# A fifth expert in the early stage, and GpSimd's work in the written order of a spectral layer with a mixture of experts

## The chip, the core and the metric

The kernel runs on one core of one Trainium2 chip. The metric is the device time of one execution in microseconds (us), the median of several runs. TensorE (PE) does the matrix products, VectorE (DVE) and ScalarE (ACT) the elementwise work, GpSimd (POOL) issues the indirect transfers (gather and scatter of rows), and SyncE (SP) issues nearly all other transfers.

## What is computed

The reference, cut to what matters. The input x has 8 sequences of 1856 rows of 256 values; there are 4 groups of 4 experts.

```python
X = np.fft.rfft(x, axis=1); Xr, Xi = X.real, X.imag
Yr = Xr @ w_r - Xi @ w_i + b_r
Yi = Xr @ w_i + Xi @ w_r + b_i
Yr, Yi = soft_threshold(Yr, 0.01), soft_threshold(Yi, 0.01)
y = np.fft.irfft(Yr + 1j * Yi, n=1856, axis=1).reshape(14848, 256)
g = argmax(y @ w_group); e = argmax(y @ w_expert[g])        # one expert of 16 for each row
out[row] = softmax_g[g] * softmax_e[e] * (relu(y[row] @ w1[g, e]) @ w2[g, e])
```

## The kernel before

Everything is done in 32-bit values. Most products are split: a value is cut into a high part (ScalarE, a cast) and a low part (VectorE, value minus high part), and three products are added up.

**First stage: four pairs of sequences.** For each pair the transforms are done as products with small tables. One letter of the string `ORDER` stands for one step of one generator, and the steps are issued in the order of the letters. `c` and `d`: first matmuls and their transposes (the first pair's eight are issued ahead of `ORDER`, by `lead_mm` and `turn_a`). `e` (`f_mm`): eight groups of matmuls with the table `T`, then `f` and `h`, the copies of the high and the low part. `j`, `k` (`m_mm`, 12 matmuls of 512 columns with the split weights `wh` and `wl`), `m`, `n`, `o`: the bias, the products and the soft threshold, fifteen of each for a pair. `r` and `s`, `v`, `w` and `x`: the inverse transform (`b_mm`, `b_turn`, `p_mm`, `p_out`, `p_turn`), which stores rows to the DRAM tensor `ys_d`. `G`, `H`, `R`: the logits and the routing, done on VectorE, twice for a pair. `S`: one scatter by GpSimd of 128 list entries to the DRAM tensor `lst`, which has a list of rows for each expert; a routing call releases 16 of them, 128 in all. From the 65th on a scatter waits for the landing of the one five before it.

**Early jobs, in the same string.** While the last pairs are still worked on, some experts take their first rows from lists that are already long enough. `l` loads raw weights (and x of the later pairs), `W` and `V` split them. `I` and `Z` load and convert the lists, `F` gathers 256 rows into a tile `xg` (two indirect transfers on GpSimd), `T` transposes them on TensorE, `X` and `Y` copy high and low part into `xth` and `xtl` of the pool `mp`. `U`, `A`, `B` are quarters of the up product and its two copies, `D`, `E`, `J` halves of the down product of 128 rows and its two copies out of PSUM, and `K` stores 128 rows to the output by an indirect transfer. `L` loads the last lists, once all scatters have landed, and `M` gathers the 384 rows of the first late job. Before, the early jobs are 8: two of 256 rows for each of the experts 0 to 3.

**The queues.** The order of TensorE, ScalarE, VectorE and SP is that of the steps (a manual schedule). GpSimd is left to the framework's scheduler. The tiles that `F` and `X` fill (`xp2`, `mp`) are allocated once the forward pools, `T` among them, are closed, which is behind the last `o`.

**Late stage.** A list of jobs is worked on one after the other: `("e", q)` is 512 rows of expert q, `("l", q)` the 384 rows behind them, `("f", i)` a flexible job of 128 rows and `("h", i)` a half job of twice 64 rows for whatever is left in the lists. Weights lie in the ring `big` (three buffers): those of the last three early experts are kept from the early stage, all others are loaded (two loads of 1 MB) and split by eight pieces on ScalarE and VectorE (`split_w`), one or two jobs ahead, as `split_at` says. In a job of kind e or l one piece follows each of eight up groups. In a half job the code is

```python
drain(half_mm(x2, wt, hts)); next(rest, None)
half_tr(hts[0], 0, hs);      next(rest, None)
half_tr(hts[1], 1, hs)
...
emit(todo, len(todo))        # all pieces of a split that falls into this job
...
x2 = half_prep(nxt) if jobs[i + 1][0] == "h" else prep(xq, nxt, jids[i + 1].n * 128)
```

where `prep` transposes the next job's rows and copies them to `xth` and `xtl`. The first thing that the next job does on TensorE is the down product of the job before.

Of the kernel before, what the change touches and what calls it, by code (L numbers as in the profile page):

```python
# [37 lines left out]
jejleffhlhekefnhmkojkfnhmojcfnhkmddjocfnhkmddjocfnhcmdkdjddokfnhmjocnmcdjcddcddeddedfohekkfnhmojkfnhmjokfnhmjokfmhnojkfn  # L38
hmjoenmefojheekkfnhmjokfnhmjokfnhmjokfnhmjorfmhnksjsorfnhmkjssormnjokssrnmojesscffdcdlhvhxcwxwkddddcnmcdljcddvlddvwxkdwo
wxxxwcmvndvdjowcxxwldGwdvxxwxvwHwRvxwxexwxeRffhwhwkxRRRRRRRGRfhnmRRjoRRRRkRHRRRRRRRkfnhmjoRRmkRnRjRoRRenRmSRRojefRfehSRh  # L40
RRkRRSRRRRRSRkRfRRmhnRRSojRkfRRnRhSmRRjkofSnhmojSRrmnojSRkssSRrmRRSnRRjesSseffRhSRkohSrfmShnksjSsorSfnhmeSsjscSovddkwSxx
# [1157 lines left out]
```

## Time and profile before

| | us |
|---|---|
| median of 3 runs | 1142.23 |
| lowest and highest | 1140.64, 1142.94 |
| the profiled execution | 1140.41 |
| its span, first to last instruction | 1138.6 |
| TensorE busy | 1102.5 |
| VectorE, ScalarE, GpSimd busy | 663.6, 547.2, 403.3 |

The time of an execution is the span and some 1.8 us around it. Busy times are those of the profiled execution. An engine's idle time counts only where another engine, and in the end the last instruction, waits for it.

### The profile page before, as it was taken

Reading aid. Unit: us, or ns where it says so; the run is one execution under the profiler, and the core shown is the slowest. Engines: PE = TensorE matmul, PEld = TensorE weight load, DVE = VectorE, ACT = ScalarE, POOL = GpSimd, SP = SyncE. Lnnn points to the kernel's source line nnn. Section 1 sums busy time; section 2 is a strip of 40 time slices with the busy share of each in tenths; the row PEclk is TensorE's granted clock in tenths of the full one; section 3 lists DMA queues with packets and bytes.
Section 4 is the critical chain, followed back from the end, with each engine's and each line's share of the span. In section 5 each row is a group of like instructions: output and inputs, shape, how many; then the busy total and the mean of one; then the engine's idle time right before and its main releaser. Section 6 shows DMA issues by size and latency. Waiting matters only on the chain. (4 is left out here: it accounts for less than half of the span.)

```text
span 1138.6 us, 19713 instructions
## 1 busy us (share of the span) xinstructions
PE 1102.5 (97%) x7282; PEld 897.1 (79%) x7282; DVE 663.6 (58%) x1453; ACT 547.2 (48%) x1234; POOL 403.3 (35%) x462
## 2 busy tenths in 40 slices
PE   8999999999997999799999999999999999999996
PEld 5686586676684789689898898888979888798785
DVE  4635777786876795265747464464554645454452
ACT  3556455545753444134636453463544645444352
POOL 3000014414447377634242333333334333343321
PEclk9999999999999999889999999999999999999999
DMA  9500610450601840413333254335425355245300
GB/s 383 173 1 1 232 65 2 141 157 2 197 28 20 230 143 24 125 47 130 129 101 123 106 190 186 122 118 204 171 75 167 121 178 183 79 170 190 117 25 24
DMA packets 42500, 138.88 MB, mean 122 GB/s; under 512 B 17462, under 2 KB 19772, under 8 KB 32034
## 3 DMA queue, kind: packets, MB, share of 16 engines
q1 hardware_dynamic: 21602, 89.22, 22.6%
q0 software_dynamic: 15904, 31.48, 8.9%
q10 hardware_dynamic: 4896, 16.91, 4.4%
q8 instruction: 58, 0.95, 0.4%
q14 instruction: 40, 0.33, 0.1%
HBM read 103.49 MB, written 35.00 MB: 122 GB/s over the span
## 5 line engine op out<-in xcount | busy, mean ns | idle before, releaser
L526 PE MATMUL py<-big,hh 128*128 128x512 f32 x824 | 298.7, 403 | 0.0
L465 PE MATMUL ph<-xth,big 128*128 128x384 f32 (+1 forms) x896 | 257.1, 363 | 5.6 <-ACT xth L452 5.6
L527 PE MATMUL py<-big,hl 128*128 128x256 f32 x824 | 232.0, 282 | 0.0
L240 POOL DMA_INDIRECT lst<-ent,sloti x128 | 129.2, 1009 | 254.0 <-DVE mx_g L156 140.8
L471 DVE SCALAR_TENSOR_TENSOR hl<-ph,hh 128x256 fp32r<-128x256 f32 x448 | 151.3, 379 | 66.1 <-ACT hh L469 64.7
L465 PEld LDWEIGHTS ph<-xth,big 128*128 128x128 f32 x896 | 166.9, 190 | 23.8 <-ACT xth L452 6.0
L526 PEld LDWEIGHTS py<-big,hh 128*128 128x128 f32 x824 | 155.3, 189 | 37.8 <-issue 3.2
L469 ACT ACTIVATE hh<-ph 128x256 fp32r<-128x256 f32 x448 | 133.9, 351 | 71.4 <-PE ph L465 70.4
L465 PE MATMUL ph<-xtl,big 128*128 128x384 f32 (+1 forms) x448 | 162.9, 364 | 0.1
L512 POOL DMA_INDIRECT out_dram<-yo,si_f x93 | 95.0, 1022 | 178.5 <-DVE yo L534 160.3
L432 POOL DMA_INDIRECT xg<-ys_d,gi_f x93 | 90.5, 973 | 186.3 <-PE pg L448 163.5
L527 PEld LDWEIGHTS py<-big,hl 128*128 128x128 f32 x824 | 155.1, 188 | 0.1
L534 DVE SCALAR_TENSOR_TENSOR yo<-py,ent_f,yo 128x256 f32<-128x256 f32 x93 | 45.0, 484 | 168.0 <-ACT yo L533 168.0
L533 ACT ACTIVATE yo<-py,ent_f 128x256 f32<-128x256 f32 x93 | 44.1, 474 | 194.1 <-PE py L527 194.1
L415 DVE TENSOR_TENSOR big<-xt,big 128x512 fp32r<-128x512 f32 x160 | 108.8, 680 | 0.0
L414 ACT CAST big<-xt 128x512 fp32r<-128x512 f32 x160 | 99.5, 622 | 0.0
L625 PE MATMUL pw<-wh,xh 128*128 128x512 f32 x240 | 98.6, 411 | 0.0
L625 PE MATMUL pw<-wl,xh 128*128 128x512 f32 x240 | 95.0, 396 | 0.0
L465 PEld LDWEIGHTS ph<-xtl,big 128*128 128x128 f32 x448 | 85.2, 190 | 8.0 <-DVE xtl L453 0.5
L609 DVE TENSOR_TENSOR xl<-bank,xh 128x512 fp32r<-128x512 f32 x60 | 40.9, 693 | 44.5 <-PE pw L625 25.0
L597 PEld LDWEIGHTS bank<-T,big 128*128 128x128 f32 x480 | 58.5, 197 | 9.4 <-issue 3.2
L625 PE MATMUL pw<-wh,xl 128*128 128x512 f32 x240 | 65.8, 396 | 0.0
(197 smaller groups left out, 1609.1 us busy)
## 6 DMA issues: line engine op xcount, KB each, us to landing
xt<-in_w_dram SPq DMA_DIRECT2D x48, 1024.0 KB, 5.0
ys_d<-ysb ACTq DMA_DIRECT2D x32, 512.0 KB, 5.1
big<-in_w_dram SPq DMA_DIRECT2D x16, 1024.0 KB, 8.3
big<-in_x_dram SPq DMA_DIRECT2D x8, 1024.0 KB, 9.4
xt<-in_x_dram SPq DMA_DIRECT2D x8, 1024.0 KB, 6.5
lst<-ent,sloti POOLq DMA_INDIRECT x128, 3.3
lst<-zero SPq DMA_DIRECT2D x1, 1920.0 KB
xg<-ys_d,gi_f POOLq DMA_INDIRECT x93, 2.8
```

Source lines behind the costliest of these rows:

```text
L240: ins = nc.gpsimd.indirect_dma_start(out=lst, out_offset=bass.IndirectOffsetOnAxis(ap=sl_, axis=0), in_=en_, in_offset=None, bounds_check= ...
L414: nc.scalar.copy(out=wt[:, 2 * i, cs], in_=raws[i][:, cs])
L415: nc.vector.tensor_tensor(out=wt[:, 2 * i + 1, cs], in0=raws[i][:, cs], in1=wt[:, 2 * i, cs].bitcast(F32), op=ALU.subtract)
L432: ins = nc.gpsimd.indirect_dma_start(out=xg[:, c, :], out_offset=None, in_=ys_d[0:rows, :], in_offset=bass.IndirectOffsetOnAxis(ap=ids.gi[ ...
L465: nc.tensor.matmul(o[:, :n], lhsT=a_[:, ch, fs], rhs=b_[:, ch, 0:n], start=k == 0, stop=k == 5)
L469: nc.scalar.activation(out=hh[:, f, :m], in_=ov, func=AF.Relu)
L471: nc.vector.scalar_tensor_tensor(out=hl[:, f, :m], in0=ov, scalar=0.0, in1=hh[:, f, :m].bitcast(F32), op0=ALU.max, op1=ALU.subtract)
L512: ins = nc.gpsimd.indirect_dma_start(out=out, out_offset=bass.IndirectOffsetOnAxis(ap=ids.si[:, t:t + 1], axis=0), in_=ysb, in_offset=None ...
L526: nc.tensor.matmul(o, lhsT=hh[:, f, ts], rhs=w2b[:, :, f, :], start=f == 0, stop=f == 7, skip_group_check=True)
L527: nc.tensor.matmul(o[:, 0:D], lhsT=hl[:, f, ts], rhs=w2h[:, f, :], start=False, stop=f == 7, skip_group_check=True)
L597: nc.tensor.matmul(o.rearrange("p (j c) -> p j c", j=4)[:, :, m * 32:m * 32 + 32], lhsT=zys[pr][:, k, bt, :, kp], rhs=T[:, 2 * k + kp, :], ...
L625: ins = nc.tensor.matmul(y, lhsT=a_[:, c * 128:c * 128 + 128], rhs=w_[:, c // 2, c % 2].rearrange("p j e -> p (j e)"), start=False, stop=a ...
```

## The change

Expert 4 becomes the fifth early expert: two more early jobs of 256 rows (`NE2`), with its weights and lists. In the late stage its 512-row job goes, the kept weights are those of experts 2, 3 and 4, so that the late jobs of experts 0 and 1 load theirs again, and the flexible and half jobs are laid between the others by a written table (`fill`). GpSimd joins the manual schedule while `ORDER` is worked through, so its instructions too come in the order of the letters. `ORDER` itself is new. The table `T` gets a pool of its own that is closed behind the last `e`, and `xp2` and `mp` are allocated there, on the other side of the memory. At the start x of the first pair is loaded in halves, all loads are issued by SP with the constants `K` last, the table is loaded and copied in other slices, part of the weights' copies moves from ScalarE to VectorE and GpSimd, and the very first `m_mm` uses `wl` last.

```diff
@@ -35,18 +35,19 @@
 ORDER = """
...
-xRRvRSmRRnRvxwokjSxwxwRwxSRRGmRnRojRRIRRReRRHRReRfRRfhhZkRRRfkRmhnRojRkRfRmhnRSRojRkmRSRnRRSRjRRRoSemRnRSRReofRfShjhkSRR
-RRRSRRRRkRSfmhnSojRSkmnSoSRmRnSRoRSrRRFRRssrSSsSTsXSYrSUsSsrASBSUsWWSsWUASWVvABSWBUWxSwVWDxASVWBwvSVDxlwSxwVvESVvxwSxwDx
-FwVwDxVJGlEKJKITHvXRRYRvwxUxwRZRwxUAxwBFURARBRDRAFRBURRRRRvFARRBvwxxDwxwRDwxRWRRDWRRRWWTGWVFXVWYWVWVEVlEJRRJUKRRKRUARBTR
-AUBFRRUHARBDSARVRXBSTRRDYSRRRURERSRDRASVRRRURSRRRDRRAFRRRTEWBWSBUWVWJSlUJAVSBDAVXBSYDVSVDESJWDWVSWVUWVSEVJUSABRRSAURBKUR
-ARKRRDXBKAYTBUKRRSDABSDEJSUSUABSDASBUESJTXDSAYBUSUSABSDABSUEJSUABSDAXBSDYSUEJKDAKBDKUKLEJUAKBDABUMDABDEJDKDEJKDEJK
...
+xRRvRmRSRnRvRxwkwoxSwxjxwRSRGmRnRRRojRRRRIReHRRReRfRRfRhZRhkRRRRRefRmShnRRkSRRojRRSRRRRSRkfRmhSnRRojSRkfRRmShnRRRSjRokRf
+RSmhnRRSjkomSnSojRSRmeRnSRfohFRkRRRRSmSnoSTrXSYSUsSsrABSUsSsrSABSUsSsrASBSUsWWSsWDASWBvWVWSVvwxWDSxWxwVSvwVwxFlDwxExwvVV
+DwxxwVGEVIJlJKKTHvXRRZYRvwxUxwFRRwxUAxwBFURARBRDRARFBURRRRvRARRBvwxxDwxwRDwxRWRRDWRRRWWTGWVFXVWYWVWVEVlEJRRJUKRRKRUARBTR
+AUBFRRUHARBDSARVRXBSTRRDYFRRRURERRDRASVRRRURSRRRDRRASRRRTSWWBEFBUWVWJlUJAVSBDAVXBSYDVSVDElSJWUWVSWVUAVSWBDVSAlBUSEWJWVSU
+AVWBSRRADRXKWBRDRWKRWRDWKRRWYUVSEVJSUVAVSBDAVBSUEVJSUABSTATXDSBYFUDABSUEJSUABSDASBUSTADSXBYSDSUSDAKBUKUAKBDAKLEBUJEKJDAK
+XBDYEJKUMUABDABUEJUKABTADXBYDUEJKUABDABUUABDABDEJKDDEJKDDEJKDEJK
 """
@@ -265,7 +266,7 @@
-    NF = 3
+    NF, NE2 = 3, 5
...
@@ -286,10 +287,10 @@
     cA = cf.tile([128, 64], F32, name="cA")
-    nc.scalar.dma_start(out=cA, in_=cst[:, _OFF["A"][0]:_OFF["A"][0] + 64])
-    nc.scalar.dma_start(out=K, in_=cst[:, CK0:CK1])
-    nc.vector.tensor_copy(out=base, in_=kc("EB"))
-    T = cf.tile([128, K1, 128], F32, name="T")
+    nc.sync.dma_start(out=cA, in_=cst[:, _OFF["A"][0]:_OFF["A"][0] + 64])
+    table_t = ExitStack()
+    ct = table_t.enter_context(tc.tile_pool(name="ct", bufs=1, side="right"))
+    T = ct.tile([128, K1, 128], F32, name="T")
     nc.gpsimd.memset(T, 0.0)
...
@@ -302,7 +303,8 @@
         for dc in range(4):
-            ins = nc.sync.dma_start(out=t[:, dc], in_=x_v[pr, dc])
+            for rs in ((slice(0, 16), slice(16, 32)) if pr == 0 else (slice(0, 32),)):
+                ins = nc.sync.dma_start(out=t[:, dc, rs], in_=x_v[pr, dc, :, rs])
         xbig[pr] = t
...
@@ -347,19 +349,20 @@
     traw = xp.tile([128, K1, 64], F32, name="xt")
-    nc.sync.dma_start(out=traw.rearrange("p k c -> p (k c)"), in_=cst[:, 0:CF1])
+    nc.sync.dma_start(out=traw[:, 0:12].rearrange("p k c -> p (k c)"), in_=cst[:, 0:12 * 64])
     def t_blocks(k):
...
-    t_blocks(slice(0, 6))
-    craw = wf.tile([128, 2 * D], F32, name="rn", bufs=1)[:, 0:128]
-    nc.sync.dma_start(out=craw, in_=cst[:, CF1:CI0])
-
+    t_blocks(slice(0, 12))
     wraw = xp.tile([128, 2, 2, D], F32, name="xt")
...
     nc.sync.dma_start(out=bias, in_=bri)
+    nc.sync.dma_start(out=traw[:, 12:].rearrange("p k c -> p (k c)"), in_=cst[:, 12 * 64:CF1])
+    craw = wf.tile([128, 2 * D], F32, name="rn", bufs=1)[:, 0:128]
+    nc.sync.dma_start(out=craw, in_=cst[:, CF1:CI0])
+    nc.sync.dma_start(out=K, in_=cst[:, CK0:CK1])
     x1 = load_x(1)
...
@@ -367,12 +370,19 @@
                             op=ALU.subtract)
-    for w_ in (wh, wl):
-        nc.scalar.activation(out=w_[:, 1, :, 0], in_=w_[:, 0, :, 1].bitcast(F32), func=AF.Copy, scale=-1.0)
-        nc.scalar.copy(out=w_[:, 1, :, 1], in_=w_[:, 0, :, 0].bitcast(F32))
-    t_blocks(slice(6, 18))
-    t_blocks(slice(18, 30))
-    nc.scalar.copy(out=sl, in_=craw)
+    with tc.issue_after(a_last.ins):
+        nc.vector.tensor_scalar_mul(out=wh[:, 1, :, 0], in0=wh[:, 0, :, 1].bitcast(F32), scalar1=-1.0)
+        nc.vector.tensor_copy(out=wh[:, 1, :, 1], in_=wh[:, 0, :, 0].bitcast(F32))
+    nc.gpsimd.tensor_scalar_mul(out=wl[:, 1, :, 0], in0=wl[:, 0, :, 1].bitcast(F32), scalar1=-1.0)
+    w_last = nc.gpsimd.tensor_copy(out=wl[:, 1, :, 1], in_=wl[:, 0, :, 0].bitcast(F32))
+    behind_w = ExitStack()
+    behind_w.enter_context(tc.issue_after(w_last.ins))
+    sl_in = nc.gpsimd.tensor_copy(out=sl, in_=craw)
+    behind_w.enter_context(tc.issue_after(sl_in.ins))
+    t_blocks(slice(12, 21))
+    t_blocks(slice(21, 30))
+    nc.gpsimd.tensor_copy(out=base, in_=kc("EB"))
+    behind_w.close()
     nlam = cf.tile([128, 1], F32, name="nlam")
...
@@ -540,7 +550,7 @@
     yp, early = [], {}
-    jobs = [(0, 0), (0, 1), (1, 0), (1, 1), (0, 2), (1, 2), (2, NF), (3, NF)]
+    jobs = [(0, 0), (0, 1), (1, 0), (1, 1), (0, 2), (1, 2)] + [(j, e) for e in range(NF, NE2) for j in (2, 3)]
     rows = [(NP - 2) * PAIR + 1] + [(NP - 1) * PAIR + 1] * 3
...
@@ -570,7 +580,7 @@
                 yield
-        for e in range(NF + 1):
+        for e in range(NE2):
             for i, src in enumerate((w1, w2)):
...
@@ -619,11 +629,11 @@
         y = psum["m", pr, k]
-        for a_, ws in ((xh, (wh, wl)), (xl, (wh,))):
+        for a_, ws in ((xh, (wh, wl)), (xl, (wh,))) if pr + k else ((xh, (wh,)), (xl, (wh,)), (xh, (wl,))):
             for c in range(4):
...
                     ins = nc.tensor.matmul(y, lhsT=a_[:, c * 128:c * 128 + 128], rhs=w_[:, c // 2, c % 2].rearrange("p j e -> p (j e)"),
-                                           start=False, stop=a_ is xl and c == 3, skip_group_check=True)
+                                           start=False, stop=a_ is (xl if pr + k else xh) and c == 3, skip_group_check=True)
         pace[:] = pace[-1:] + [ins.ins.name]
...
@@ -729,14 +739,14 @@
-    @steps_of(range(NF + 1), range(2), range(4))
+    @steps_of(range(NE2), range(2), range(4))
     def w_high(e, i, c):
...
-    @steps_of(range(NF + 1), range(2), range(4))
+    @steps_of(range(NE2), range(2), range(4))
     def w_low(e, i, c):
...
@@ -747,11 +757,12 @@
     def list_load(j):
-        lists[j] = t = list_tiles("ab"[j], 6 + 4 * j)
+        lists[j] = t = list_tiles("ab"[j], 6 + 8 * j)
         nc.sync.dma_start(out=t.ent[:, 0:6].rearrange("p (e c) k -> p e c k", e=NF), in_=list_rows(0, NF, j * LEV, LEV))
...
             for h in range(2):
-                nc.sync.dma_start(out=t.ent[:, 6 + 2 * h:8 + 2 * h].unsqueeze(1), in_=list_rows(NF, 1, h * LEV, LEV))
+                nc.sync.dma_start(out=t.ent[:, 6 + 4 * h:10 + 4 * h].rearrange("p (e c) k -> p e c k", e=2),
+                                  in_=list_rows(NF, 2, h * LEV, LEV))
...
@@ -760,7 +771,8 @@
             for h in range(2):
-                lev[2 + h, NF] = lists[j].cut(6 + 2 * h, 8 + 2 * h)
+                for e in range(2):
+                    lev[2 + h, NF + e] = lists[j].cut(6 + 4 * h + 2 * e, 8 + 4 * h + 2 * e)
...
@@ -851,7 +863,7 @@
         head = list_tiles("h", w - 4)
-        nc.sync.dma_start(out=head.ent.unsqueeze(1), in_=list_rows(1, 1, EARLY, STAT - EARLY))
+        nc.sync.dma_start(out=head.ent.unsqueeze(1), in_=list_rows(NF - 1, 1, EARLY, STAT - EARLY))
         final = list_tiles("f", NE * w)
...
@@ -860,7 +872,7 @@
     def first_rows(_):
-        behind(nc.gpsimd.tensor_copy(out=first[1].gi, in_=first[1].ent[:, :, 0]), "stores that are ready go first")
+        nc.gpsimd.tensor_copy(out=first[1].gi, in_=first[1].ent[:, :, 0])
         first.append(fetch(xp2, first[1], 3))
...
@@ -873,15 +885,18 @@
     by_hand.enter_context(tc.manual_schedule(engines=engines))
-    with ExitStack() as ph:
-        done = 0
+    with ExitStack() as ph, tc.manual_schedule(engines={mybir.EngineType.Pool}):
+        done, turned = 0, 0
         for c in ORDER.replace("\n", ""):
...
             done += c == "o"
+            turned += c == "e"
+            if c == "e" and turned == NP * 8:
+                table_t.close()
+                xp2 = ctx.enter_context(tc.tile_pool(name="xp2", bufs=3, side="right"))
+                early["mp"] = ph.enter_context(tc.tile_pool(name="mp", bufs=1, side="right"))
             if c == "o" and done == NP * 15:
                 fwd.close()
-                xp2 = ctx.enter_context(tc.tile_pool(name="xp2", bufs=3, side="right"))
-                early["mp"] = ph.enter_context(tc.tile_pool(name="mp", bufs=1))
                 yp.append(ph.enter_context(tc.tile_pool(name="yp", bufs=4)))
...
@@ -1055,13 +1070,14 @@
-    jobs = [("l", e) for e in range(1, NF + 1)] + [("e", NF + 1), ("l", NF + 1), ("l", 0)]
-    flex = iter([("f", 0), ("f", 1), ("h", 0), ("f", 2), ("h", 1), ("f", 3), ("f", 4), ("h", 2), ("f", 5), ("h", 3), ("f", 6)])
-    for e in range(NF + 2, NE):
-        jobs += [("e", e), ("l", e), next(flex)]
+    jobs = [("l", e) for e in range(NF - 1, NE2)]
+    fill = {NE2: [("l", 0)], NE2 + 1: [("l", 1)], 7: [("f", 0)], 8: [("h", 0), ("f", 1)], 9: [("f", 2)], 10: [("h", 1)],
+            11: [("f", 3)], 12: [("h", 2), ("f", 4)], 13: [("f", 5)], 14: [("h", 3)], 15: [("f", 6)]}
+    for e in range(NE2, NE):
+        jobs += [("e", e), ("l", e)] + fill[e]
     jobs[-2:] = jobs[:-3:-1]
-    loads = [j for j, (kind, q) in enumerate(jobs) if kind in "ef" or (kind, q) == ("l", 0)]
-    split_at = {j - 1 if j in (NF, len(jobs) - 2) else j - 2: j for j in loads}
+    loads = [j for j, (kind, q) in enumerate(jobs) if kind in "ef" or (kind == "l" and q < NF - 1)]
+    split_at = {j - 1 if j in (3, len(jobs) - 2) else j - 2: j for j in loads}
     raws, jids, jw = {}, {}, {}
...
     def dma_next():
```

## Rows read from the trace of the kernel before

**Rows 1.** The page's head and its part 1: the span, and TensorE's busy time with its share of the span and its instructions.

```profile
span 1138.6 us, 19713 instructions
PE 1102.5 (97%) x7282; PEld 897.1 (79%) x7282; DVE 663.6 (58%) x1453; ACT 547.2 (48%) x1234; POOL 403.3 (35%) x462
```

**Rows 2.** Busy time by stages (start:end, length, then PE, PEld, DVE, ACT and POOL, each with its number of instructions; then the granted clock, the DMA share and GB/s).

```profile
0.00:18.09 18.09, 13.82 (x91) 5.75 (x91) 9.83 (x21) 2.23 (x4) 5.57 (x10) 1.00 0.91 360
...
343.00:359.00 16.00, 9.97 (x106) 3.54 (x104) 9.05 (x14) 1.85 (x3) 12.07 (x13) 0.89 0.20 34
...
380.00:402.00 22.00, 19.52 (x200) 15.18 (x196) 16.57 (x41) 11.87 (x23) 7.80 (x11) 1.00 0.75 215
402.00:474.50 72.50, 72.33 (x548) 66.51 (x537) 44.85 (x93) 27.81 (x54) 52.56 (x55) 1.00 0.29 82
474.50:491.50 17.00, 7.65 (x24) 6.53 (x24) 3.62 (x12) 2.44 (x7) 12.89 (x19) 0.60 0.40 141
491.50:1128.00 636.50, 636.12 (x3554) 552.32 (x3553) 339.59 (x826) 310.28 (x811) 216.41 (x260) 1.00 0.38 131
```

**Rows 3.** Whom TensorE waited for in the whole run (us in total, times, longest).

```profile
PE ph L465 <- ACT xth L452: 5.6, 1, 5.6
...
PE ph L797 <- DVE hl L809: 1.4, 1, 1.4
PE bank L776 <- DMA xg<-ys_d,gi_b: 1.1, 1, 1.1
```

**Rows 4.** Timeline of TensorE, first and last of 24 up matmuls of an early job (line 797), and first and last of 48 of a late job (line 465).

```profile
461.85 0.29 PE L797 MATMUL ph<-xth,big 128*128 128x256 f32 x1
...
464.48 0.28 PE L797 MATMUL ph<-xth,big 128*128 128x256 f32 x1
...
744.28 0.50 PE L465 MATMUL ph<-xth,big 128*128 128x512 f32 x1
...
755.16 0.39 PE L465 MATMUL ph<-xth,big 128*128 128x512 f32 x1
```

**Rows 5.** The split of raw weights, high part on ScalarE and low part on VectorE, all pieces of 128x512 (duration in ns: least, median, most).

```profile
L414 ACT CAST big<-xt x160: 621/622/639, 523.7 to 1093.3; 128x512 fp32r<-128x512 f32 x160
L415 DVE TENSOR_TENSOR big<-xt,big x160: 675/680/685, 524.3 to 1094.2; 128x512 fp32r<-128x512 f32 x160
```

**Rows 6.** Timelines around the end of the early jobs: TensorE, VectorE, GpSimd, ScalarE (start, length, instruction, and in brackets the idle time before it and what ended it).

```profile
473.93 0.28 PE L823 MATMUL bank<-big,hl 128*128 128x256 f32 x1
...
474.28 0.28 PE L823 MATMUL bank<-big,hl 128*128 128x256 f32 x1
478.18 1.67 PE L448 MATMUL pg<-K,xg 128*128 128x128 f32 x6 [3.62 <-DMA xg<-ys_d,gi_h]
485.49 0.69 PE L465 MATMUL ph<-xth,big 128*128 128x384 f32 x1 [5.64 <-ACT xth L452]
475.10 0.48 DVE L840 SCALAR_TENSOR_TENSOR yo<-bank,ent_b,yo 128x256 f32<-128x256 f32 x1 [2.31 <-ACT yo L833]
463.56 0.98 POOL L240 DMA_INDIRECT lst<-ent,sloti  x1 [0.30 <-issue]
...
473.70 1.00 POOL L432 DMA_INDIRECT xg<-ys_d,gi_h  x1 [0.27 <-POOL gi_h L863]
...
481.91 1.07 POOL L512 DMA_INDIRECT out_dram<-yo,si_b  x1 [0.17 <-issue]
484.58 0.86 ACT L452 CAST xth<-pg 128x512 fp32r<-128x512 f32 x2 [9.51 <-DMA out_dram<-yo,si_b]
```

**Rows 7.** One microsecond of the busy time by stages, columns as in rows 2.

```profile
490.00:491.00 1.00, 1.00 (x5) 1.00 (x4) 0.54 (x2) 0.55 (x2) 0.55 (x2) 0.50 0.45 127
```

**Rows 8.** Timeline of TensorE after the last m_mm of pair 3.

```profile
346.19 2.79 PE L655 MATMUL bank<-big,CI 32*64 32x512 f32 x36 [2.05 <-DVE big L641]
...
354.92 1.08 PE L776 MATMUL bank<-K,xg 128*128 128x128 f32 x4 [3.43 <-DMA xg<-ys_d,gi_a]
```

**Rows 9.** Timeline of GpSimd at the same place: the first scatter that the third pair's routing releases, and the first gather behind it.

```profile
328.98 1.37 POOL L240 DMA_INDIRECT lst<-ent,sloti  x1 [6.63 <-DVE sloti L227]
...
350.08 1.00 POOL L432 DMA_INDIRECT xg<-ys_d,gi_a  x1 [0.30 <-issue]
```

**Rows 10.** Two of the waits of GpSimd in the whole run (us in total, times, longest).

```profile
POOL lst L240 <- DMA lst<-ent,sloti: 13.3, 10, 3.6
POOL gi_b L254 <- DMA ent_b<-lst: 12.1, 1, 12.1
```

**Rows 11.** Timelines at the start: TensorE, VectorE, GpSimd.

```profile
7.05 2.81 PE L326 MATMUL bank<-big,cA 64*64 64x512 f32 x24
8.78 0.17 DVE L291 COPY base<-K 128x16 f32<-128x16 f32 x1 [7.33 <-DMA K<-in_cst_dram]
8.86 9.68 DVE L330 STREAM_TRANSPOSE big<-bank 128x512 f32<-128x512 f32 x16
20.75 2.40 POOL L368 TENSOR_TENSOR wl<-xt,wh 128x1024 fp32r<-128x1024 f32 x1
```

**Rows 12.** Timelines in the first half job: TensorE, ScalarE, VectorE.

```profile
740.68 3.67 PE L1052 MATMUL py<-big,hh 128*64 128x256 f32 x32
739.47 0.47 ACT L533 ACTIVATE yo<-py,ent_f 128x256 f32<-128x256 f32 x1 [2.85 <-PE py L527]
740.38 0.68 DVE L1046 COPY hh<-ph 128x512 f32<-128x512 f32 x1
```

More of the change, by code (lines that the diff above doesn't have):

```diff
@@ L37 @@
 ORDER = """
[L38 to L41, printed above, removed]
@@ L42 @@
-wSvfmhvwxnSxkwxwowSxjvfmhvSwxnvxwoGSwjSkHSxxwxwRSvwxRmvxwcwSxxwclwdkdSRnddjxSRRRcmRRRGlSddRRRoRcRnRHcjdedlddeRfRRfhhcRRo
-cdkdlddRRRRefnhmRRojkRRRRRefRSRnhkmRRRRjoSRRRRkfRnSRhmRRjoRSkRfRnRRhmRSRjRRRkRfRmShoRRneRSmRjRRkfRShRRoSnefojhnSkmjoSrfm
-hSnksjSsorSfmhnksjSsSormnSojkssSrnSmojeWsWSWseffhSWhvWVWvxwSVwkxwxWxSwVWvVfVlmvSxwhwkxwSxnxwojVvSfVmGhwVnSlojSvxxwkxwSHw
-xRRvRSmRRnRvxwokjSxwxwRwxSRRGmRnRojRRIRRReRRHRReRfRRfhhZkRRRfkRmhnRojRkRfRmhnRSRojRkmRSRnRRSRjRRRoSemRnRSRReofRfShjhkSRR
-RRRSRRRRkRSfmhnSojRSkmnSoSRmRnSRoRSrRRFRRssrSSsSTsXSYrSUsSsrASBSUsWWSsWUASWVvABSWBUWxSwVWDxASVWBwvSVDxlwSxwVvESVvxwSxwDx
@@ L47 @@
-FwVwDxVJGlEKJKITHvXRRYRvwxUxwRZRwxUAxwBFURARBRDRAFRBURRRRRvFARRBvwxxDwxwRDwxRWRRDWRRRWWTGWVFXVWYWVWVEVlEJRRJUKRRKRUARBTR
-AUBFRRUHARBDSARVRXBSTRRDYSRRRURERSRDRASVRRRURSRRRDRRAFRRRTEWBWSBUWVWJSlUJAVSBDAVXBSYDVSVDESJWDWVSWVUWVSEVJUSABRRSAURBKUR
-ARKRRDXBKAYTBUKRRSDABSDEJSUSUABSDASBUESJTXDSAYBUSUSABSDABSUEJSUABSDAXBSDYSUEJKDAKBDKUKLEJUAKBDABUMDABDEJDKDEJKDEJK
+jejeffhlhkkfnlhmojefmhnkojcfnhcmdkdjddocfmhcndcdjdkdddocmncdjcddedddefohekkfmhnojefnhmkojkfnhmojkfmhnojkfnhmojkfmhnojkfn
+hmjoemnefojheekkfnhmjokfnhmjokfmhnojkfmhnojrfmhnksjsorfnhmksjsormnojkssrmnojesscffdcdlhvhxcwxwkddddcmncdljcddvlddvwdvxow
@@ new lines @@
+xkwxxwxwwxcmGdndjovHcxwvxwldvwdRxvxwxewRwxxwefxfhwhGRRRRRRRRRRkRHRRRRRRRRkRfRmhnRjokfnhmojRRmkRnRRjoRRemRnSRRojefRfehSRh
+RRkRRSRRRRRSRkRfRRmhnRRSojRkfRRmRhSnRRjkofSmhnojSRRmrRnRRjSoksSsRrmRSnRRojesSseffhShkSrfSmhnksjSsoSrfmhneSsjscSovddkwSxx
+wSvfmhvwxSnxkwxwowSxjvfmhSvwxnvxwoGSwjSkxSHwxwxSxvwRRmvxwSwcxxcwldwSkdRnddjxSRRRcmRRRGlSddRRRoRcRnRHcjdedlddeoffhhcRRcdd
+klddRRRReRRfRmnhRRjokRRRRRefRShmknRRojRSRRRRkRfRmhSnRojRkSfhmnRRRRSjRokfRmhnSRRRjRokRmRSRnRjoRSRmeRnRRjSRefofhhkSRRRSrfm
+hSnksjsSorfSmhnksjSsoSrmnojkSssSrmnSojeWsWSWseffhWhvSWVWvxwVwkSxwxWxwSVWvVfVlmvxSwhwkxwxnSxwojVvfVSmGhwVnlSojvxSxwkxwHwS
```

## The prediction

> **What bounds the kernel now.** I read the page first. TensorE is busy for 1102.5 of the 1138.6 us of the span [rows 1], so the end is set by TensorE, and another engine counts only where TensorE waits for it. The second view is therefore the table by stages [rows 2]: subtract the busy time from the length of each stage. From 491.5 to 1128 nothing is idle (636.50 against 636.12), so a better order can win nothing there, though it can lose. The idle time lies in four places: 4.3 us before 18.09, 6.0 us between 343 and 359, 2.5 us between 380 and 402, and 9.3 us between 474.5 and 491.5, where the granted clock is also only 0.60. The third view, the waits of TensorE, names what each place waits for [rows 3]. Timelines of the four places then give the chains.
>
> **Part 1, the fifth expert itself: nothing.** Two jobs of 256 rows move in front of the last lists; one job of 512 rows goes behind them. In an early job the up matmuls of 256 columns start every (464.48 - 461.85) / 23 = 0.114 us [rows 4], so two jobs of 48 take 10.98 us. In the late stage 48 matmuls of 512 columns start every (755.16 - 744.28) / 47 = 0.231 us [rows 4], or 11.1 us. The down matmuls have the same shapes in both. About 23 us of TensorE work move from one stage to the other at the same price. The early weights cost one more pair of 1 MB loads and eight splits on ScalarE and VectorE, but experts 0 and 1 are now both loaded twice while expert 4 is loaded once less late: the late stage keeps 20 loads. In 402 to 474.5 ScalarE is busy 27.81 and VectorE 44.85 of 72.5 us [rows 2], so I cost the splits at 0. Without that cover they would cost 8 x 0.68 = 5.4 us [rows 5].
>
> **Part 2, the seam between the stages: -7.3 us.** Today the last scatter starts at 463.56, the gather of the head list at 473.70, and TensorE is out of work at 474.56 [rows 6]. The transposes run at 478.18. The first late activation then waits until 484.58, and its releaser is a store to out_dram: the last early output started at 481.91, behind three gathers and the index arithmetic, and the tile that the activation writes lies where the early outputs lay. TensorE starts again at 485.49, 10.93 us after its last early matmul. After the change some 23 us more of matmuls stand behind the last scatter, and the order on GpSimd is fixed with the gather (M) six stores before the end. The chain from last scatter to transposes took 478.18 - 463.56 = 14.6 us. In the new order I count 18 quarter-steps (U or D, each 12 matmuls of 0.114 us or 4 pairs of 474.28 - 473.93 = 0.35 us, so 1.4 us) between M and the end: 25 us of cover, and the gather is hidden. What stays is the last store. VectorE ends 1.02 us after the last matmul (475.10 + 0.48 - 474.56), GpSimd takes 0.30 us to issue, store to release is 484.58 - 481.91 = 2.67, and release to matmul is 485.49 - 484.58 = 0.91 [rows 6]. That is 4.90 us, a saving of 6.0. The clock adds to it. It is still 0.50 at 490 [rows 7], so the old gap is followed by 6.0 us at half speed, which lose 3.0. The shorter gap at 352 shows a mean of 0.89 over 16 us [rows 2]: 16 x 0.11 / 0.5 = 3.5 us at half speed, 1.7 lost. I take 1.7, because 4.90 us with transposes in it is nearer to that gap, and so 1.3 us more saved. The bounds are 6.0 (clock as before) and 13.1 (no gap left: 10.93 - 0.85 of transposes at full speed + 3.0).
>
> The Trainium skill, "TensorE: Matmul & The Clock Gate", section "HAM oscillation — how this bites in real kernels", says that an array kept waiting between bursts drops to half clock and pays for getting it back each time. By that rule alone the new gap would cost what the old one did, 3.0 us, and the sum below would be 1.3 us smaller. The half clock after both gaps agrees with it.
>
> **Part 3, the step from pair 3's spectrum to its inverse: -5.4 us.** TensorE waits 2.05 us for the last subtraction (r needs all of z) and 3.43 us for the first early job's rows [rows 8]. With 0.5 us between, that is 6.0 us, and 1.7 for the clock: 7.8. Those rows come late because the tiles for them could be allocated only when the forward pools closed, and because 16 scatters, released at 328.98, stand ahead of them on GpSimd until 350.08 [rows 9]. Now the table of f is a pool of its own, closed after the last f_mm, and F follows 14 scatters. In ORDER the routing that releases those scatters stands two m_mm groups earlier, 2 x 12 x 0.23 = 5.5 us [rows 4]. So the gather starts at 328.98 - 5.5 + 14 x 1.3 = 341.7 and lands as before 4.84 us later (354.92 - 350.08), at 346.5, just where r could start (346.19). T stands ahead of the first r and fills 0.6 of the 2.05. U stands between the r, so that no r waits for VectorE. One small loss is new: the last f_mm is followed directly by its m_mm, which waits about 0.9 us for the copy (0.6 and the release). 7.8 - 1.45 - 0.9 = 5.4. The bounds are 7.0 and a loss of 2 (third rival).
>
> **Part 4, small gains: -2.4 us.** Between 380 and 402 TensorE waits 1.4 for VectorE and 1.1 for a gather [rows 3], and GpSimd has stood 12.1 us for that list [rows 10]. In the new order the list's load stands ahead of a 1 MB weight load on SP's queue. I take -1.5 of at most -2.5, and at least 0. At the start VectorE's first transpose, 8.86, follows a copy that waited for K [rows 11]. That copy leaves VectorE for GpSimd. The first eight of 24 lead matmuls that take 2.81 us from 7.05 are done at 8.0, so the sixteen transposes start 0.9 earlier and the first f_mm with them: -0.9, or 0 if x comes no sooner. The negated weights that move from ScalarE to VectorE and GpSimd cost 0: on GpSimd a subtraction of 1024 columns takes 2.40 us [rows 11], so the two moves of 512 take at most 2.4. The table's first 12 blocks are copied first, the other 18 behind, and the first m_mm uses wl in its last four matmuls. Without that cover up to 2.4 us are lost.
>
> **Part 5, weight splits inside half jobs: +5.0 us.** The new job list puts a flex job right behind half jobs 0 and 2, and the split of the next expert then falls into the half job. In all jobs before it fell into e or l, one piece per up group. In a half job all eight pieces are issued at once, ahead of the copies (xth, xtl) that the flex job needs. From the half job at 732 [rows 12]: ScalarE is free at 739.94 and VectorE at 741.06. Eight pieces take 8 x 0.62 = 5.0 and 8 x 0.68 = 5.4 us [rows 5] (a little less when they follow closely), and the two copies behind them end near 745 and 746.5. TensorE has only the half job's down to do: 3.67 us, begun near 740.0 since a flex job has two transposes instead of eight. It stops at 743.7, does two matmuls (0.46) once xth is there, and waits for xtl: 746.5 - 743.7 - 0.46 = 2.3, with 0.2 for the second flex transpose. 2.5 us, twice. The weights themselves are in time: their load can start when the l job's pieces are done, more than 15 us before. The bounds are 0 (other work covers it) and 6.
>
> **Sum.** -7.3 - 5.4 - 1.5 - 0.9 + 5.0 = -10.1 us. The profiled execution took 1140.41 us, 1.8 more than its span. The median of the runs is 1142.23 and a run has come as low as 1140.64, so I take the sum off the median: 1132.1 us.
>
> **Rivals.** (1) The seam closes altogether: the late tiles no longer lie on the last outputs, since the pool mp moves to the other side, and ScalarE and VectorE find time for the splits. For it: only one tile's place decides it. Against: four output buffers of 1 KB now lie where mp lay, under about the same place. -13.1 - 5.4 - 2.4 = -20.9: 1121.3. (2) The seam stays as it is: the last store again waits behind index arithmetic or gathers and part 2 gives nothing. For it: that is what 481.91 shows [rows 6]. Against: the stores are now in a written order. -2.8: 1139.4. (3) T waits. It stands before every r, where the old order had two of them first. If the routing chain is no earlier, the gather starts at 347.5 and lands at 352.3; idle from 343.9 to there plus the clock is about 10 us instead of 7.8. Part 3 is then +2 and the sum -2.7: 1139.5. (4) Slower: the same place, with GpSimd's written order holding the gather behind a scatter that waits for the landing of one five before it. Such waits add up to 13.3 us [rows 10]. Each us past 352.3 costs one; from a landing at 355.0 the kernel is slower than before, and with all of the 13.3 us it takes 1152. Against: the waits sat mostly where stores filled the queues, not here.
>
> **How the numbers follow.** A measurement of this kernel tells about 0.2% (2.3 us) from no change. Chances: the forecast 0.55 (its own range 1127 to 1138), (1) 0.12, (2) 0.12, (3) 0.10, (4) 0.08, others 0.03. The range of 8 in 10 reaches to rivals 2 and 3 above, and part of the way to rival 1 below: 1123 to 1140. Faster than 1139.9: 0.53 + 0.12 + 0.07 + 0.06 = 0.78; within 0.2%: 0.10, half of (2) and (3) with the edge of the forecast; slower 0.12, (4) and the others.
>
> **What would show it.** Right: no wait of TensorE for a gather at the seam, a gap near 5 us there that ends on a store, T and r together near 345, two new waits of about 2.5 us for xtl behind half jobs, and no change elsewhere after 500. Wrong: a seam as wide as before, T waiting for xg, no idle in the flex jobs, or GpSimd standing before a store while TensorE waits for a gather.

## The result: slower by half a per cent

The changed kernel takes 1147.01 us (median of 11 runs, 1143.17 to 1151.91), the kernel before 1141.98 us beside it (1138.62 to 1143.63). The ratio is 1.0055 with a 95% interval of 1.0043 to 1.0067. The prediction, 1132.1 us and faster, was wrong. A later comparison gave 1.0059 (1.0039 to 1.0080).

The head of the page of the changed kernel, to be read against [rows 1]: the span is 6.6 us longer, and TensorE is still busy for 97% of it.

```profile
span 1145.2 us, 19789 instructions
...
PE 1109.3 (97%) x7330; PEld 903.5 (79%) x7330; DVE 671.7 (59%) x1454; ACT 547.6 (48%) x1229; POOL 408.0 (36%) x466
```

Busy time by stages of the changed kernel, columns as in [rows 2]:

```profile
144.00:157.00 13.00, 8.73 (x83) 5.58 (x82) 4.70 (x13) 2.56 (x6) 0.00 (x0) 0.74 0.42 170
...
345.00:360.00 15.00, 12.05 (x91) 7.16 (x97) 8.16 (x15) 4.47 (x8) 11.35 (x13) 0.89 0.11 18
...
380.00:402.00 22.00, 21.90 (x230) 17.50 (x232) 18.24 (x45) 11.75 (x23) 9.22 (x14) 1.00 0.84 299
...
436.00:448.00 12.00, 8.44 (x38) 6.92 (x37) 6.98 (x14) 5.71 (x11) 6.33 (x7) 0.72 0.30 53
...
505.00:516.00 11.00, 8.84 (x42) 7.71 (x41) 3.43 (x11) 2.91 (x8) 8.03 (x12) 0.84 0.23 73
...
775.00:790.00 15.00, 12.85 (x83) 9.66 (x83) 9.24 (x16) 8.43 (x17) 7.84 (x9) 1.00 0.53 180
```

And whom TensorE waited for in the whole run, against [rows 3]:

```profile
PE bank L716 <- ACT ysb L696: 4.4, 2, 4.3
PE bank L833 <- ACT hh L817: 3.4, 1, 3.4
PE bank L788 <- DMA xg<-ys_d,gi_a: 2.3, 1, 2.3
PE ph L494 <- DVE xtl L463: 2.2, 2, 1.1
...
PE ph L494 <- ACT xth L462: 1.4, 2, 0.7
...
PE pg L458 <- DVE ones_f L1004: 1.1, 1, 1.1
PE ph L475 <- ACT xth L462: 0.7, 1, 0.7
```

The old waits at the seam have shrunk (L465 for xth, 5.6 us, is now L475, 0.7). The place 380 to 402 is nearly full, and in 505 to 516 TensorE idles 2.16 us. Two waits are new at the top: g_mm (L716) at 150 us, whose like in the kernel before was 0.7 us long, and a down matmul (L833) at 440 us. Each is followed by half clock.

To compare places I add the idle time of TensorE and the time that its work lost at half clock (busy time times 1 minus the granted clock, in steps of 1 us). Below are all runs of this study by that measure, in us for each stretch, with the ratio to the kernel before that was timed beside them. The seam is the passage from the early to the late stage. Base and edits of each run are told further down:

| kernel | ratio (95%) | 0-20 | 144-157 | 340-366 | 366-402 | 428-463 | seam | half jobs |
|---|---|---|---|---|---|---|---|---|
| before | 1 | 4.3 | 0 | 7.7 | 2.5 | 0 | 13.2 | 0 |
| changed | 1.0055 (1.0043-1.0067) | 5.5 | 7.3 | 4.7 | 0.1 | 6.8 | 3.8 | 4.3 |
| changed, again | 1.0059 (1.0039-1.0080) | 5.8 | 7.0 | 7.4 | 2.2 | 10.2 | 2.2 | 4.3 |
| old order at 150 | 1.0011 (0.9998-1.0024) | 5.4 | 0.3 | 6.5 | 0 | 9.9 | 2.2 | 4.3 |
| late splits | 1.0084 (1.0071-1.0097) | 5.3 | 5.8 | 6.4 | 0.9 | 9.4 | 2.2 | 5.7 |
| flex splits | 1.0031 (1.0014-1.0049) | 6.1 | 6.6 | 7.4 | 2.5 | 8.4 | 3.7 | 1.7 |
| all three | 0.9984 (0.9973-0.9994) | 5.5 | 0 | 6.1 | 3.0 | 9.0 | 2.2 | 1.7 |
| outputs early | 0.9928 (0.9908-0.9947) | 6.0 | 0 | 6.2 | 0.6 | 3.6 | 2.2 | 1.7 |
| outputs early, late splits | 0.9897 (0.9882-0.9912) | 5.6 | 0 | 7.5 | 1.3 | 0.8 | 2.2 | 1.7 |
| the same, again | 0.9914 (0.9896-0.9932) | 5.3 | 0 | 6.0 | 1.9 | 0.3 | 2.2 | 1.7 |
| only the place at 430 | 0.9990 (0.9978-1.0003) | 5.5 | 7.2 | 4.7 | 0 | 0.2 | 3.8 | 7.4 |
| mp back on the left | 0.9946 (0.9930-0.9962) | 6.2 | 0 | 6.4 | 1.4 | 2.1 | 8.0 | 1.7 |
| old start | 0.9924 (0.9907-0.9942) | 6.0 | 0 | 4.9 | 1.7 | 0.4 | 3.8 | 1.7 |
| gather early | 0.9945 (0.9928-0.9962) | 5.4 | 0 | 2.0 | 9.1 | 0.2 | 3.8 | 1.7 |

The changed kernel lost 45.1 us in all, the kernel before 41.7. The remaining 3.2 us of the longer span are TensorE work at full speed (1100.1 against 1096.9 us). From the last m_mm of pair 3 to the first late up matmul that work grew by 25.6 us, from there to the end it fell by 21.8, and ahead of it it fell by 0.6. The edited kernels show the same two stages within 2 us, so it is no accident of one trace, but which matmuls take longer stays open.

### The profile page after: what moved, and what is told of

Same layout as the page of the kernel before. It is cut to its first block, busy times and chain, and to the rows that moved or that the text cites. A ratio compares the mean times of both kernels' runs of the same rounds, so it can differ in the third digit from the quotient of the medians.

```text
span 1145.2 us, 19789 instructions
## 1 busy us (share of the span) xinstructions
PE 1109.3 (97%) x7330; PEld 903.5 (79%) x7330; DVE 671.7 (59%) x1454; ACT 547.6 (48%) x1229; POOL 408.0 (36%) x466
## 5 line engine op out<-in xcount | busy, mean ns | idle before, releaser
L536 PE MATMUL py<-big,hh 128*128 128x512 f32 x792 | 286.8, 402 | 0.0
L475 PE MATMUL ph<-xth,big 128*128 128x384 f32 (+1 forms) x864 | 245.7, 360 | 0.7 <-ACT xth L462 0.7
L537 PE MATMUL py<-big,hl 128*128 128x256 f32 x792 | 222.6, 281 | 0.0
L481 DVE SCALAR_TENSOR_TENSOR hl<-ph,hh 128x256 fp32r<-128x256 f32 (+1 forms) x432 | 145.4, 378 | 60.3 <-ACT hh L479 58.9
L536 PEld LDWEIGHTS py<-big,hh 128*128 128x128 f32 x792 | 149.0, 188 | 36.5 <-issue 3.2
L475 PEld LDWEIGHTS ph<-xth,big 128*128 128x128 f32 x864 | 159.9, 189 | 16.7 <-ACT xth L462 1.0
L479 ACT ACTIVATE hh<-ph 128x256 fp32r<-128x256 f32 (+1 forms) x432 | 128.6, 350 | 71.2 <-PE ph L475 70.4
L475 PE MATMUL ph<-xtl,big 128*128 128x384 f32 (+1 forms) x432 | 156.0, 361 | 0.3 <-DVE xtl L463 0.3
L537 PEld LDWEIGHTS py<-big,hl 128*128 128x128 f32 x792 | 148.9, 188 | 0.1
L475 PEld LDWEIGHTS ph<-xtl,big 128*128 128x128 f32 x432 | 81.7, 189 | 7.7 <-DVE xtl L463 0.6
L614 ACT CAST xh<-bank 128x512 fp32r<-128x512 f32 x60 | 34.3, 587 | 65.4 <-PE pw L635 49.5
```

The costliest lines, as they stand in the source:

```text
L475: nc.tensor.matmul(o[:, :n], lhsT=a_[:, ch, fs], rhs=b_[:, ch, 0:n], start=k == 0, stop=k == 5)
L479: nc.scalar.activation(out=hh[:, f, :m], in_=ov, func=AF.Relu)
L481: nc.vector.scalar_tensor_tensor(out=hl[:, f, :m], in0=ov, scalar=0.0, in1=hh[:, f, :m].bitcast(F32), op0=ALU.max, op1=ALU.subtract)
L536: nc.tensor.matmul(o, lhsT=hh[:, f, ts], rhs=w2b[:, :, f, :], start=f == 0, stop=f == 7, skip_group_check=True)
L537: nc.tensor.matmul(o[:, 0:D], lhsT=hl[:, f, ts], rhs=w2h[:, f, :], start=False, stop=f == 7, skip_group_check=True)
```

## The experiments

**The wait at 150 us.** The waits lead from g_mm to ScalarE, from there to a store. Below are the timeline of ScalarE in the changed kernel, the time from issue to landing of the load of SP at 138.90 and of the store at 139.42, and the DMA queues in 141 to 144 and in 144 to 147 (queue, packets, MB, share; q1 carries SP's transfers, q10 ScalarE's):

```profile
139.42 0.33 ACTq L699 DMA_DIRECT2D ys_d<-ysb  x1
...
148.22 0.58 ACT L696 COPY ysb<-bank 128x512 f32<-128x512 f32 x1 [4.77 <-DMA ys_d<-ysb]
```

```profile
xt<-in_x_dram SPq DMA_DIRECT2D x1, 1024.0 KB, 6.6
ys_d<-ysb ACTq DMA_DIRECT2D x1, 512.0 KB, 8.7
```

```profile
q1 hardware_dynamic: 103, 0.83, 94.0%
q10 hardware_dynamic: 2, 0.01, 0.7%
```

```profile
q10 hardware_dynamic: 286, 1.07, 87.7%
q1 hardware_dynamic: 25, 0.09, 8.6%
```

The load was issued 0.52 us ahead of the store, and its bytes went first: 0.83 MB of the load and 0.01 MB of stores up to 144, then the reverse. The store landed 8.7 us after its issue, and the third of three output buffers waited for it.

```diff
 ORDER: 88 steps that run at 97 to 160 us
-dvxowxkwxxwxwwxcmGdndjovHcxwvxwldvwdRxvxw
+xkdwowxxxwcmvndvdjowcxxwldGwdvxxwxvwHwRvx
 ...
```

> Edit: 88 steps of the order (those that run at 97 to 160 us) are put back as they were before; all else is the changed kernel. Theory: TensorE's new wait at 150 us (4.27 us, and 3.0 lost at half clock behind it) comes from the order alone: the load of 1 MB is issued at 138.90, 0.5 us ahead of the store of 139.42, whose landing then takes 8.7 us, and ScalarE's copy waits 4.77 us for the buffer under that store. With the old order the place loses 2.0 in 100 to 144 instead of 1.0, and nothing behind it: 1147.0 - 7.3 + 1.0 = 1140.7 us, no wait of ScalarE over 1 us for a store before 160. Rival: the wait follows from the new start or the table's new pool, and stands in the old order too: 1147 us.

Measured: 1.0011, about 5 us less than the changed kernel's 1.0055 where 6.3 was expected, and 0.3 us lost at 144 to 157. A wait of ScalarE for a store is left, but of 2.20 us. The place at 440 lost 9.9 us in this trace, where the changed kernel lost 6.8. The theory holds in the main: the order alone made this stall. That it was the load just ahead of the store is read from the rows above; no run moves the load by itself.

**The half jobs.** VectorE in the changed kernel behind the first of the two half jobs, as [rows 12] shows it without a split:

```profile
775.96 4.89 DVE L425 TENSOR_TENSOR big<-xt,big 128x512 fp32r<-128x512 f32 x8
780.77 0.41 DVE L463 TENSOR_TENSOR xtl<-pg,xth 128x256 fp32r<-128x256 f32 x1
```

```diff
+        if kind == "h":
+            todo, held = [], todo
         emit(todo, len(todo))
 ...
             x2 = half_prep(nxt) if jobs[i + 1][0] == "h" else prep(xq, nxt, jids[i + 1].n * 128)
+        if kind == "h":
+            emit(held, 4)
```

Four pieces are issued behind the copies, the other four inside the next job's up matmuls, two by two.

> Edit: the job list stays; in the two half jobs that carry a weight split, four of the eight pieces are issued behind the copies for the next job's rows, and four inside that flex job. Theory (part 5 of the prediction): the two losses of 2.15 and 2.16 us at 775 to 790 and 975 to 990 go, nothing else changes: 1147.0 - 4.3 = 1142.7 us, and no wait of TensorE for xtl behind a half job. Rival: the pieces hold the flex job's own relu and copies instead, and the loss only moves by some us: 1146 to 1148.

Measured: 1.0031, 0.24% or 2.7 us below the changed kernel, though the two intervals touch. In the trace the two places lose 1.7 instead of 4.3 us, which is 2.6. No wait for xtl is left behind the half jobs; what stays are waits of 0.4 us for ht and hl. The theory holds for 2.6 of 4.3 us.

**The wait at 440 us, first theory.** ScalarE stands before the first weight piece of the fifth expert, and the relu copies of the job in hand behind it:

```profile
438.93 1.14 ACT L747 CAST big<-xt 128x512 fp32r<-128x512 f32 x2 [5.74 <-DMA xt<-in_w_dram]
439.98 0.59 ACT L817 ACTIVATE hh<-ph 128x512 fp32r<-128x512 f32 x1
...
448.38 0.48 ACT L845 ACTIVATE yo<-bank,ent_a 128x256 f32<-128x256 f32 x1 [3.75 <-DMA out_dram<-yo,si_b]
```

```diff
 ORDER, W and V: a piece's high part (ScalarE) and low part (VectorE)
-...AlBUSEWJWVSUAVWBSRRADRXKWBRDRWKRWRDWKRRWYUVSEVJSUVAVSBDAVBSUEVJS...
+...AlBUSEJSUABSRRADRXKBRDRKRRDKRRYUSEJSUASBDWABSUWVEJSUWVABSTATXDWVSB...
```

> Edit: in the order, the 16 weight pieces (W, V) of the fifth expert stand about 9 to 12 us later, behind the 20th D; all else is the changed kernel. Theory: TensorE's wait at 437.2 to 440.6 (3.4 us, 2.9 more at half clock) comes from the first of these pieces, which holds ScalarE from 433.2 to 438.93 until its 1 MB load has landed (11.4 us after issue), and the relu copies of the second-last expert behind it. With the pieces later the load has landed when they come: 1147.0 - 6.4 = 1140.6 us. Rival: whatever makes the load land late at that time (GpSimd's scatter waits 6.0 us for a landing there too) holds TensorE by another way, a gather or a store: the wait moves, 1147 us. Second rival: the raw buffers come free 10 us later, and the late stage's first loads with them: a new wait at 500 to 530.

Measured: 1.0084, no gain. The piece no longer waits, yet 9.4 us are lost at the same place. My theory fell; the first rival names what the trace shows. Below is ScalarE in the run with late splits, then GpSimd there:

```profile
450.45 0.47 ACT L845 ACTIVATE yo<-bank,ent_a 128x256 f32<-128x256 f32 x1 [12.75 <-DMA out_dram<-yo,si_b]
```

```profile
434.04 0.98 POOL L241 DMA_INDIRECT lst<-ent,sloti  x1 [0.30 <-issue]
439.27 0.98 POOL L241 DMA_INDIRECT lst<-ent,sloti  x1 [4.25 <-DMA lst<-ent,sloti]
...
444.42 0.99 POOL L522 DMA_INDIRECT out_dram<-yo,si_b  x1 [0.30 <-issue]
```

The early outputs have four tiles. In the written order their stores (K) stand behind ten scatters (S), and one of these waits 4.25 us for the landing of another. All four tiles are full, ScalarE waits 12.75 us for the next one, and TensorE waits for a relu copy that stands behind it on ScalarE. The last line of ScalarE's timeline of the changed kernel, above the edit, showed the same, a wait of 3.75 us, in the shadow of the other stall. The kernel before, where GpSimd's order was not written, stored at 431.36, 432.65, 439.10 and 440.39.

**All three edits** together show how the stalls add:

> Edit: the three edits together. Theory: three stalls of separate causes, so the gains add: 1147.0 - 6.3 - 6.4 - 4.3 = 1130.0 us, which is the predicted 1132.1 with part 5 gone and a seam that gives 9.4 instead of 7.3. Rival: the stalls are linked by the time at which DMA transfers meet, and with one gone another comes: 1135 to 1142.

Measured: 0.9984. The old order and the flex splits give what they gave alone (1.0055 - 0.0044 - 0.0024 = 0.9987), and the late splits nothing, 9.0 us being lost at 428 to 463. The time is far from the 1130.0 expected, near the rival.

**The stores early.** Seven stores move forward in the order, first without and then with the late splits:

```diff
 ORDER, K: the store of an early output, S: one scatter
-...XBSYDVSVDElSJWUWVSWVUAVSWBDVSAlBUSEWJ...RXKWBRDRWKRWRDWK...
+...XBSYDVSKVDElSJWUWVSKWVUAVSWBDVSAlBUSKEWJ...RXWBRDRWRWRDW...
```

> Edit: on the kernel with the old order at 97 to 160 us and the moved half-job splits, seven output stores (K, the 5th to 11th) stand in GpSimd's order 5 to 16 scatters earlier, near the outputs that they store; the weight pieces of the fifth expert stay where the change has them. Theory (new, since later weight pieces did not remove the stall): two things hold TensorE at 437 to 458. The first weight piece waits for its load, and the ring of four output tiles is full, since four stores stand behind ten scatters, one of which waits 4 to 6 us for a landing; ScalarE then waits for a store (12.75 us at 450 in the run with later pieces). With the stores early alone, the wait for the load stays (3 to 6 us with the clock), and the wait of ScalarE for a store goes: about 1143. Rival: the stores are not the cause, loss in 430 to 460 stays 8 to 9 us: 1146.

> Edit: the run with all three edits, and the seven output stores early as well. Theory: with both causes gone nothing is left in 430 to 460; the run with three edits lost 5.34 + 3.01 there, so 1143.1 - 8.3 = 1134.8 us, and no wait of ScalarE over 1 us for a store. Rival one: only the stores matter, then this run and the one with the early stores alone take the same time. Rival two: neither matters, a third wait comes: 1141 to 1144.

Measured: 0.9928, where about 1143 us had been expected (0.998 of the kernel before as timed then), and 0.9897 (1134.56 against 1146.11 us). Below is the busy time at 428 to 460 with all three edits, then with the stores early as well:

```profile
428.00:460.00 32.00, 25.99 (x168) 24.21 (x168) 15.48 (x28) 11.43 (x23) 21.50 (x22) 0.89 0.49 103
```

```profile
428.00:460.00 32.00, 31.20 (x222) 28.78 (x221) 21.65 (x38) 16.26 (x31) 22.06 (x22) 1.00 0.43 85
```

The same 32 us hold 222 matmuls instead of 168. Two holds stood in a row: the late splits are worth nothing alone (9.4 us lost), the early stores leave 3.6, both leave 0.8. With the stores early, the splits in their old place still make ScalarE wait 3.14 and 4.15 us for the load. By time the stores are worth 0.87% beside the late splits (0.9984 to 0.9897) and 0.59% without them (from 0.9987, which is worked out and was not run, to 0.9928). What the late splits then add isn't settled by time: 0.9928 goes to 0.9897, or to 0.9914 in the second comparison told below, and the intervals overlap.

These two moves alone, on the changed kernel:

> Edit: the changed kernel with nothing but the two moves near 430 us: the seven output stores early and the fifth expert's weight pieces late. Theory: the loss at 437 to 458 goes by itself; going by the ratios of the runs with three edits (0.9984) and with the stores early as well (0.9897), about 0.8% less than the changed kernel's 1.0059: 0.997 to 0.999, and the waits at 150 us and behind the half jobs stay. Rival: the place at 430 was late only because the kernel had lost 7 us at 150, and without the old order there it gets worse in another way: 1.003 or more.

Measured: 0.9990, 0.65% below the changed kernel, with 0.2 us lost at 428 to 463 and the stall at 150 still there. The theory holds: moving 23 letters takes back what the change had lost.

The kernel with all four edits is faster than the kernel before and the changed kernel: 0.9897, and 0.9914 in a second comparison.

> The run with early stores and later pieces once more, as the base of the early gather: its ratio of 0.9897 comes again.

**The seam.** One part of the change undone, on that kernel:

mp opens again where the forward pools close, not at the last f_mm:

```diff
-                early["mp"] = ph.enter_context(tc.tile_pool(name="mp", bufs=1, side="right"))
+                early["mp"] = ph.enter_context(tc.tile_pool(name="mp", bufs=1))
```

> Edit: as the run with early stores and later pieces, but the pool of the early experts' turned rows (mp) lies where it lay before the change, below the early outputs. Theory: the seam is short (2.15 us idle, 1.6 at half clock) because the late tiles no longer lie on outputs whose stores are still on their way; with mp back, ScalarE's first late copy waits for the last store again, and the seam costs about what the prediction gave it, 4.9 + 1.7 us: 2.5 to 3.5 us more than with mp on the right. Rival: the fifth expert's cover alone closes the seam, mp is of no account: same time within 1 us.

Measured: 0.9946 against 0.9897, 5.6 us. Below is ScalarE's first late copy with mp on the left, then on the right, and TensorE's first late up matmul with mp on the left:

```profile
502.17 0.86 ACT L462 CAST xth<-pg 128x512 fp32r<-128x512 f32 x2 [4.16 <-DMA out_dram<-yo,si_b]
```

```profile
501.14 0.86 ACT L462 CAST xth<-pg 128x512 fp32r<-128x512 f32 x2 [1.27 <-PE pg L458]
```

```profile
503.08 0.69 PE L475 MATMUL ph<-xth,big 128*128 128x384 f32 x1 [3.62 <-ACT xth L462]
```

The theory was right and its price too low: TensorE loses 4.80 us idle and 3.15 at half clock, against 2.16 and none. From the last early matmul to this one 5.58 us pass, with mp on the right 2.69.

**The start.**

> Edit: as the run with early stores and later pieces, but the start (first loads, the copies and negations of the weights, the first 89 steps of the order) is that of the kernel before. Theory: the first f_mm starts at 18.1 instead of 18.5, TensorE idles 4.3 us instead of 5.5 before 19, and three f_mm lie in front of the first m_mm: 1 us less or the same. Rival (the prediction's -0.9): the new start is the better one by 1 us.

Measured: 0.9924 against 0.9897 and 0.9914 of its base; the intervals overlap. The old start idles 0.5 us less, but loses 1.7 us at half clock by 22. Neither start is shown to be the better one.

**The pair-3 step.**

```diff
 ORDER, F: the gather of an early job
-...komSnSojRSRmeRnSRfohFRk...
+...komSnojRRmeFRnRfohSSSRk...
```

> Edit: as the run with early stores and later pieces, and the gather of the first early job (F) stands right behind the last f_mm in the order, three scatters earlier on GpSimd. Theory: T waits for that gather alone (3.84 us at 345 to 349, 2.95 more lost at half clock); its tile lies in the table's place and is free once the last f_mm ends at 341.2, so the gather can start there instead of 344.58 and land at about 345.4. Then r waits for the last subtraction (346.95 + release), and 341 to 355 loses about 2.1 us idle instead of 4.4 and less clock: 2 to 4 us less than the run that it starts from. Rival: the three scatters behind the gather delay the later gathers by as much: no change.

Measured: 0.9945, 0.3 to 0.5% slower than its base. Below is the busy time of the run with the early gather, then the matmul that pays for it:

```profile
340.00:356.00 16.00, 14.05 (x148) 8.47 (x146) 11.29 (x17) 4.80 (x8) 11.57 (x12) 1.00 0.08 18
376.00:390.00 14.00, 8.66 (x69) 5.50 (x62) 5.80 (x14) 2.90 (x6) 4.47 (x9) 0.76 0.94 240
```

```profile
382.08 0.66 PE L788 MATMUL bank<-K,xg 128*128 128x128 f32 x2 [5.12 <-DMA xg<-ys_d,gi_a]
```

The step itself gains as expected: 2.0 us lost instead of 7.5 and 6.0. But TensorE then comes 4 to 5 us sooner to a later T, whose gather GpSimd issues at 372.22 instead of 371.06 behind the same scatters, and loses 8.5 us there. The gain was given back, as the rival said, and more.

**The changed kernel again.**

> The changed kernel as it is, on the chip of this call. Theory: the waits at 146 to 157 and 437 to 458 follow from the written order and come again at the same places, with a loss of 6 to 9 us each; the ratio to the kernel before is 1.0055 as measured first. Rival: they were an accident of one execution's DMA times, and another profiled execution shows them elsewhere or not at all.

Measured: 1.0059; 7.0 us lost at 146 to 156, and 10.2 at 437 to 463. The first stall repeats to 0.01 us (4.26 idle). The second stands at its place, but its size moves from run to run (6.8 and 10.2 us for the same kernel).

## Why the prediction was wrong

**Part 1, the fifth expert itself: 0. The failed step.** The splits were costed at 0 because ScalarE was busy 27.81 of 72.5 us there. A share of busy time doesn't price a piece that waits, on an engine that works in order, for a load: the first piece stood 5.74 us. Nor did I follow the outputs: part 2 looked at GpSimd's last stores and not at those of the jobs before, which the written order puts behind ten scatters. Together they cost 6.8 us in the first trace, and by the two moves alone 0.65% of the time (7.4 us). Nor was the price of the moved matmuls quite the same in both stages, as part 1 had it: TensorE's own work grew by 25.6 us early against 21.8 saved late, 3.2 us over the whole run. Why stays open.

**Missing: the stall at 150.** The 88 steps there were in the diff, and the prediction gave them no term, up or down. They cost 7.3 - 1.0 = 6.3 us in the trace (100 to 144 improved by 1.0), and 5 us by time. The first view of the prediction lists the places that idle and says of 491.5 to 1128 alone that a new order can lose there. It can wherever it differs.

**Part 2, the seam: -7.3, measured 13.2 - 3.8 = -9.4.** The cover by the added matmuls was right: no gather is waited for. Wrong was that the last store would hold ScalarE. The first rival named why not: mp has moved. The run with mp on the left is the predicted seam: 5.58 us from the last early matmul to the first late one, where 4.90 was worked out. Its clock term, 1.7, was too small (3.15). The Trainium skill, "TensorE: Matmul & The Clock Gate", section "HAM oscillation — how this bites in real kernels", says that waits between bursts of matmuls bring half clock back each time. The gap of 5.58 us agrees with it. The gap of 2.69 us, with 2.16 of them idle, was followed by 1.5 to 1.7 us lost at half clock in five of the runs above, and by none in seven, so at this gap the prediction's way of reading a clock loss off the width of a gap gives nothing firm.

**Part 3: -5.4, measured -3.1.** The gather started at 349.56, not at 341.7, since the scatters in front of it began at 330.75, not at 323.5. That is the stall at 150 carried on. Where that stall is gone the scatters begin at 325.14, and the gather still goes at 344.58. The clock took 1.5 to 3.0 us beside the idle time in all runs with this order, and the part gave between 0.3 and 3.1.

**Part 4: -2.4.** 380 to 402 fell from 2.5 to 0.1 in the first trace (-1.5 predicted), but with the same gather order other traces lose up to 3.0 between 366 and 402, so this gain isn't firm. The start gave no -0.9. VectorE's first transpose did begin earlier, at 8.16 instead of 8.86, but TensorE then waited 1.16 us for a later piece of x, the first f_mm began at 18.54 instead of 18.09, and 0 to 20 lost 5.5 us instead of 4.3: +1.2.

**Part 5, half jobs: +5.0, measured +4.3** by the mechanism told: eight pieces at once stand ahead of xth and xtl.

**The sum** of the parts that were foreseen is -9.4 - 3.1 - 2.4 + 1.2 + 4.3 = -9.4, against -10.1 predicted. That they agree so well is in part luck: part 2 gave more than foreseen, parts 3 and 4 less. The two stalls that had no term, 6.3 and 6.8, and the 3.2 of longer work turn it into +6.9, against 6.6 of the span; the rest are small places. The range failed because every rival sat at a place that the prediction had already priced; none asked what else the 1,504 steps moved. Rival 4 came nearest: GpSimd's written order did stand behind a scatter that waited for a landing, but at 434 and ahead of output stores, not at pair 3's gather.

## What to carry to other kernels

A written order fixes more than the step that one follows. For each moved step, look at what the engine has queued behind it and which landing it waits for; a low busy share is no cover for a wait. Count every ring of buffers whose release lies on another engine's queue: here four output tiles stood behind ten scatters. When a removed wait gives nothing, look for the second hold behind it before dropping the theory: the late splits alone gave nothing here, and without them the early stores still left 3.6 us.
